# Writing out the whole issue order of an attention and ELU-MLP kernel, in half-pair steps

## The chip, the cores and the metric

The kernel runs on one core of a Trainium2 chip. A core has a matrix engine (TensorE, "PE" in the profile, with its weight loads shown apart as "PEld"), a vector engine (VectorE, "DVE"), a scalar engine (ScalarE, "ACT"), GpSimd ("POOL") and an engine that here issues most DMAs (SyncE, "SP"). Each engine works through its own queue in order. The metric is device time in microseconds (us), less is better; before the change the median of three runs is 621.48 us (619.19 to 624.78). A profile is one execution; its span leaves out a little at both ends.

## The reference

Attention is a gated linear recurrence over 768 tokens, for 4 batches and 8 heads of 48; its output, heads side by side (3072 tokens of 384), goes through a two-layer MLP with ELU.

```python
q, k, v, f_logit: (4, 8, 768, 48) float32;  w_in: (384, 2048), w_out: (2048, 384) float64

f = 1 / (1 + exp(-f_logit))
for t in range(768):
    state = f[t][:, None] * state + outer(k[t], v[t])      # per batch and head, 48 x 48
    y[t] = q[t] @ state
x = y, heads next to each other                            # (3072, 384)
h = x @ w_in
g = where(h > 0, h, exp(min(h, 0)) - 1)
out = g @ w_out
```

The weights come as float64, since a float32 array times a NumPy scalar gives float64. The kernel turns them into float32 itself.

## The kernel before, in words

**Units.** The 3072 tokens are cut into 12 units (`NU`) of 256 tokens, three per batch. For each unit the kernel does the attention and then the MLP. The MLP of unit m and the attention of unit m+1 run side by side. `fast` is the function that runs here; `general` (line 17) is a slower way for extreme gate values, entered at the end only if a flag asks for it (line 949).

**Attention.** A unit is cut into four chunks of 64 tokens. `gates` (545) takes the exponential of the negated gate logits on ScalarE and adds 1, and has GpSimd put restart values at chunk starts. `growth` (557) runs a scan on VectorE per pair of heads, which gives the running product of 1/f, and multiplies k by it on GpSimd. `decays` (569) takes the reciprocal on VectorE and multiplies q by it. A unit has four pairs of heads, so four times scan, reciprocal and product. `transposed` (595) transposes k on TensorE, `advance` (634) computes what each chunk adds to the state, with `stepped` (603) carrying the state over on VectorE; `scores` (614) is q times k within chunks, masked on VectorE; `outputs` (651) multiplies scores by v; `carried` (670) adds q times the state, and has six small DMAs on SP move the fourth pair's rows into the gaps of the other three (694), after which the tile `xt` holds the unit's x.

**MLP.** 2048 hidden columns are 16 blocks (`NFT`) or 8 pairs (`NP`). `up` (783) does a pair: 12 instructions on TensorE into a two-buffer PSUM tile `psH`, relu and exp on ScalarE, and the ELU's last step on VectorE (797). `down` (809) multiplies by w_out. In units 0 and 1 (`DIRECT`) it does so directly, with 8 instructions of 384 columns (818). From unit 2 on it is a Winograd scheme of 7 products of 2x2 blocks instead of 8: 14 instructions of 192 columns (840), four sums of the activations per pair on VectorE (807), and at the end of the unit a few additions on VectorE (850) and one DMA out (857). The sums of weight blocks that the scheme needs are made once by `combine` (771), after unit 0.

**Weights.** Each of 16 parts (768 KB; a pair's columns of w_in, or its rows of w_out) is fetched by `fetch` (470) into one of seven slots of `area`, and made float32 by integer arithmetic: `rounding` (487) on ScalarE scales the low words into a rounding term, in place, and `convert` (495) does three operations on VectorE: shift and mask of the high words into `bits` (508), an integer add of the rounding term (512), and a combination with sign and top exponent bits that writes the float32 tile (518). Later the weights are read once more and `check` (527) takes minimum and maximum (536), for the flag.

**Order.** The opening and unit 0 are issued in the order of the program text (`manual_schedule`, 426). After unit 0 `start.close()` (935) ends that, and for units 1 to 11 the framework's scheduler orders the instructions of each engine by its own costs. Within a unit, the loop at 915 goes over 16 half-pairs: even ones do an up, odd ones the down of the pair before. `attention` (759) hangs TensorE's parts for the next unit on half-pairs 3, 6, 8, 10 and 12 (one later in unit 0), and `prepare` (582) gives one piece of gates, growth or decays per half-pair, so all of a unit's attention is prepared within the unit before it.

Of the kernel before, what the change touches and what calls it, by code (L numbers as in the profile page):

```python
# [10 lines left out]
U32 = mybir.dt.uint32  # L11
AF = mybir.ActivationFunctionType
# [343 lines left out]
def fast(ctx: ExitStack, tc: tile.TileContext, q, k, v, f_logit, w_in, w_out, out, flag):  # L356
# [14 lines left out]

# [17 lines left out]
    DIRECT = 2  # L389
    AHEAD = 7  # L390
# [35 lines left out]
    start.enter_context(tc.manual_schedule())  # L426
    blank(0, nc.vector, nc.gpsimd)
    load(0, nc.scalar)

    ident = cst.tile([128, 128], FP32, name="ident")  # L430
# [14 lines left out]
    for i in range(1, NB):  # L445
        blank(i, nc.gpsimd)
    between = cst.tile([128, NW, HP], FP32, name="between")
    fine = cst.tile([128, HP, NC], FP32, name="fine")
    nc.vector.memset(fine[:], 1.0)
    py = ps.tile([128, HP, W], FP32, tag="a1", name="psY")  # L450
    nc.vector.memset(py[:], 0.0)
# [3 lines left out]
    wi = cst.tile([128, NKT, DFF], FP32, name="wi")  # L455
# [11 lines left out]
    parts = [(0, 0), *((j + i, 1 - i) for j in range(NFT // 2 - 1) for i in (1, 0)), (NFT // 2 - 1, 1)]  # L467

    def fetch(n):
# [4 lines left out]
        to = wo[:, 2 * j : 2 * j + 2] if out_ else wi[:, :, c]  # L474
# [12 lines left out]
    def rounding(n):  # L487

        if wide and n < NFT:
            raw = raws[n]  # L490
            nc.scalar.activation(
                raw.bitcast(I32)[:, 0::2], raw.bitcast(U32)[:, 0::2], AF.Copy, scale=2.0**-29
            )

    def convert(n):

# [3 lines left out]
        j, out_ = parts[n]  # L503
        raw = raws.pop(n)
        rnd = raw.bitcast(I32)[:, 0::2]
        hi = raw.bitcast(I32)[:, 1::2]
        bits = sb.tile([128, 2 * DM], I32, tag="bits", name=f"bits{n}", bufs=1)
# [4 lines left out]
        nc.vector.tensor_tensor(out=bits[:], in0=bits[:], in1=rnd, op=ALU.add)  # L512
        to = wo[:, 2 * j : 2 * j + 2] if out_ else wi[:, :, j * 256 : (j + 1) * 256]
# [3 lines left out]

        nc.vector.scalar_tensor_tensor(
# [7 lines left out]

    def check(n):

        if not wide:
            return  # L530
        w = w_out if n % 2 else w_in
        flat = w.rearrange("a b -> (a b)").rearrange("(p i f) -> i p f", p=128, f=2 * DM)
        raw = area[:, 4 + n % (AHEAD - 4)]
        nc.sync.dma_start(out=raw, in_=flat[n // 2])
        for i, op in enumerate((ALU.min, ALU.max)):
            nc.vector.tensor_reduce(  # L536
                out=spans[:, i, n : n + 1], in_=raw.bitcast(FP32)[:, 1::2], axis=mybir.AxisListType.X,
                op=op, apply_absolute_value=True,
            )


    restart = cst.tile([128, HP, U], FP32, name="restart")
    nc.gpsimd.memset(restart[:], 0.0)

    def gates(u):

        f = qkf[u % NB]["f"]
        pts[u] = sb.tile([128, HP, U], FP32, tag="p", name=f"p{u}")
        for i in range(2):
            a = f[:, 2 * i : 2 * i + 2] if u else f[:, :, i * W : (i + 1) * W]  # L550
            nc.scalar.activation(a, a, AF.Exp, scale=-1.0)
            nc.scalar.activation(a, a, AF.Copy, bias=1.0)
            if u:
                nc.gpsimd.tensor_copy(restart[:, 2 * i : 2 * i + 2, ::C], a[:, :, ::C])
                nc.gpsimd.memset(a[:, :, ::C], 0.0)  # L555

    def growth(u, pairs, cols):

        t = qkf[u % NB]
        for p in range(pairs.start, pairs.stop):  # L560
            a = t["f"][:, p, cols]
            nc.vector.tensor_tensor_scan(  # L562
                out=a, data0=a, data1=restart[:, p, cols] if u else a,
                initial=1.0, op0=ALU.mult, op1=ALU.max,
            )
        k_ = t["k"][:, pairs, cols]
        nc.gpsimd.tensor_tensor(out=k_, in0=k_, in1=t["f"][:, pairs, cols], op=ALU.mult)  # L567

    def decays(u, pairs, cols):

        t = qkf[u % NB]
        nc.vector.reciprocal(pts[u][:, pairs, cols], t["f"][:, pairs, cols])  # L572
        q_ = t["q"][:, pairs, cols]
        nc.vector.tensor_tensor(out=q_, in0=q_, in1=pts[u][:, pairs, cols], op=ALU.mult)
# [7 lines left out]
    def prepare(u):  # L582

        gates(u)
        yield
        for i in range(2):
            for p in range(2 * i, 2 * i + 2):
                growth(u, slice(p, p + 1), slice(0, U))
            yield
        for p in range(HP):  # L590
            decays(u, slice(p, p + 1), slice(0, U))
            yield
        watch(u)

    def transposed(u, w, bank):

        pt = ps.tile([128, HP, 128], FP32, tag=bank, name=f"psT{u}_{w}")
        for p in range(HP):
            nc.tensor.transpose(pt[:, p, :], in_=qkf[u % NB]["k"][:, p, w * W : (w + 1) * W], identity=ident[:])  # L599
        kns[u, w] = sb.tile([128, HP, 128], FP32, tag="kn", name=f"kn{u}_{w}")  # L600
        nc.scalar.copy(kns[u, w][:], pt[:])

    def stepped(u, c, pu, end):

        s = sb.tile([128, HP, D], FP32, tag="state", name=f"state{u}_{c}", bufs=6)
        now = pu
        if u % UPB or c:
# [375 lines left out]
```

## Time and profile before

| | |
|---|---|
| runs | 619.19, 621.48, 624.78 us |
| profiled execution | 622.88 us, its span 620.9 us, mean granted clock of TensorE 0.966 |
| busy: TensorE, VectorE, ScalarE, GpSimd | 572.7, 413.4, 196.7, 59.1 us |
| first up-projection begins, last down ends | 33.9 us, 611.8 us |
| DMA moved | 50.78 MB, 187 to 261 GB/s in most slices of the first 60 us |

How to read the lines that follow. A line of groups gives the kernel's line, engine, operation, what is written and read, the shape, the count, then the busy sum in us and the mean of one in ns, then the idle time before it with what ended that. A line of the timeline gives start and length in us; instructions that follow each other closely are merged, with their count. The chain of waits is the series of pieces of work that led to the last instruction. The row PEclk, where it is shown, is the clock that TensorE was granted, in tenths.

### The profile page before, as it was taken

The page shows a single profiled execution, that of the slowest core. Times are in us where ns is not written, and L with a number is a line of the kernel's source. Part 1 is how long each engine was busy: PE and PEld are TensorE (multiplying, and loading weights), DVE is VectorE, ACT ScalarE, POOL GpSimd, SP SyncE. Part 2 cuts the span into 40 slices and gives each one's busy share as a digit, 9 for nine tenths or more (in the row PEclk, how much of TensorE's full clock was granted, in tenths as well). Part 3 has the DMA queues.
Part 4 walks back from the last instruction along what each step waited for, and adds up shares of the span by engine and source line. Part 5 has one row for each costly group of instructions (what it writes and reads, how often), then busy time and mean ns, then how long its engine had stood idle before and what let it go on. Part 6 is the DMA issues. An engine that isn't in the chain of part 4 may idle for free.

```text
span 620.9 us, 13009 instructions
## 1 busy us (share of the span) xinstructions
PE 572.7 (92%) x5402; PEld 499.3 (80%) x5402; DVE 413.4 (67%) x839; ACT 196.7 (32%) x352; POOL 59.1 (10%) x115
## 2 busy tenths in 40 slices
PE   2787699898999899999999999999999999999994
PEld 1556476675879899899999899999989989999993
DVE  6879999998699976667576675483493443532432
ACT  2254244233413323325314322323313313323220
POOL 7021003223001001002002001000000000000000
PEclk9887799979999999999999999999999999999998
DMA  8999709338682403003112112002000000000000
GB/s 187 250 253 246 184 3 197 64 84 261 221 279 79 159 32 87 26 26 86 44 28 69 41 27 59 27 26 59 25 2 8 26 2 8 26 3 8 27 0 31
DMA packets 31781, 50.78 MB, mean 82 GB/s; under 512 B 3520, under 2 KB 24544, under 8 KB 31712
## 3 DMA queue, kind: packets, MB, share of 16 engines
q1 hardware_dynamic: 31088, 49.26, 30.0%
q8 instruction: 44, 0.72, 0.5%
q10 hardware_dynamic: 624, 0.59, 0.4%
q14 instruction: 25, 0.20, 0.1%
HBM read 44.04 MB, written 4.72 MB: 79 GB/s over the span
## 4 chain that ended last, share of the span: by engine, by line
PE 69%; DVE 14%; DMA 8%; issue 5%; POOL 1%; ACT 1%; SPq 0%; DVEq 0%; POOLq 0%
PE psH L790 33%; PE psM L840 25%; DMA area<-in_moe_w_in_dram 5%; DVE p L572 4%; PE psM L818 3%; DVE f L562 3%; DMA q<-in_q_dram 2%; PE psS L624 2%; DVE spans L536 2%; PE psU_a L643 2%; DVE gg L797 2%; PE psY L661 1%; PE psT L599 1%; PE psY L681 1%; DMA f<-in_f_logit_dram 1%
## 5 line engine op out<-in xcount | busy, mean ns | idle before, releaser
L790 PE MATMUL psH<-xt,wi 128*128 128x256 f32 x1152 | 275.2, 390 | 0.0
L790 PEld LDWEIGHTS psH<-xt,wi 128*128 128x128 f32 x1152 | 218.8, 194 | 32.2
L797 DVE SCALAR_TENSOR_TENSOR gg<-gg,psH 128x512 f32<-128x512 f32 x96 | 64.8, 676 | 162.5 <-ACT gg L796 132.4
L795 ACT ACTIVATE gg<-psH 128x512 f32<-128x512 f32 x96 | 57.2, 596 | 323.6 <-PE psH L790 299.2
L840 PE MATMUL psM<-area,sums 128*128 128x192 f32 x480 | 91.3, 326 | 0.0
L572 DVE RECIPROCAL p<-f 128x256 f32<-128x256 f32 x48 | 82.5, 1734 | 0.3
L840 PEld LDWEIGHTS psM<-area,sums 128*128 128x128 f32 x480 | 80.2, 190 | 0.0
L840 PE MATMUL psM<-wo,gg 128*128 128x192 f32 x320 | 65.5, 327 | 3.5 <-DVE gg L797 3.5
L840 PEld LDWEIGHTS psM<-wo,gg 128*128 128x128 f32 x320 | 55.4, 190 | 8.3 <-DVE gg L797 4.7
L567 POOL TENSOR_TENSOR k<-k,f 128x256 f32<-128x256 f32 x48 | 39.7, 853 | 230.0 <-DMA k<-in_k_dram 196.0
L796 ACT ACTIVATE gg<-gg 128x512 f32<-128x512 f32 x96 | 60.6, 631 | 2.6
L818 PE MATMUL psM<-wo,gg 128*128 128x384 f32 x128 | 47.3, 516 | 3.3 <-DVE gg L797 3.3
L807 DVE TENSOR_TENSOR sums<-gg 128x128 f32<-128x128 f32 x160 | 42.5, 306 | 2.0
L818 PEld LDWEIGHTS psM<-wo,gg 128*128 128x128 f32 x128 | 25.3, 203 | 19.4 <-DVE gg L797 4.1
L562 DVE TENSOR_TENSOR_SCAN f<-f,restart 128x256 f32<-128x256 f32 x44 | 31.6, 761 | 11.6 <-POOL f L555 11.6
L840 PE MATMUL psM<-area,gg 128*128 128x192 f32 x160 | 39.1, 326 | 0.0
L840 PE MATMUL psM<-wo,sums 128*128 128x192 f32 x160 | 39.1, 326 | 0.0
L599 PE MATMUL psT<-ident,k 128*128 128x128 f32 x96 | 15.3, 298 | 18.3 <-POOL k L567 18.3
L536 DVE TENSOR_REDUCE spans<-area 128x1 f32<-128x768 f32 x32 | 29.3, 942 | 2.0 <-DMA area<-in_moe_w_out_dram 1.7
L599 PEld LDWEIGHTS psT<-ident,k 128*128 128x128 f32 x96 | 12.0, 151 | 21.3 <-POOL k L567 20.0
L840 PEld LDWEIGHTS psM<-area,gg 128*128 128x128 f32 x160 | 28.1, 190 | 0.1
L840 PEld LDWEIGHTS psM<-wo,sums 128*128 128x128 f32 x160 | 28.1, 190 | 0.0
(79 smaller groups left out, 427.5 us busy)
## 6 DMA issues: line engine op xcount, KB each, us to landing
area<-in_moe_w_out_dram SPq DMA_DIRECT2D x16, 768.0 KB, 7.7
area<-in_moe_w_in_dram SPq DMA_DIRECT2D x8, 768.0 KB, 5.9
v<-in_v_dram SPq DMA_DIRECT2D x12, 384.0 KB, 4.4
area<-in_moe_w_in_dram SPq DMA_DIRECT2D x16, 288.0 KB, 9.0
f<-in_f_logit_dram SPq DMA_DIRECT2D x23, 192.0 KB, 4.3
k<-in_k_dram SPq DMA_DIRECT2D x23, 192.0 KB, 3.9
q<-in_q_dram SPq DMA_DIRECT2D x23, 192.0 KB, 3.6
out_dram<-o SPq DMA_DIRECT2D x10, 384.0 KB, 2.5
```

The source lines that it names most:

```text
L536: nc.vector.tensor_reduce(out=spans[:, i, n : n + 1], in_=raw.bitcast(FP32)[:, 1::2], axis=mybir.AxisListType.X, op=op, apply_absolute_val ...
L562: nc.vector.tensor_tensor_scan(out=a, data0=a, data1=restart[:, p, cols] if u else a, initial=1.0, op0=ALU.mult, op1=ALU.max,)
L567: nc.gpsimd.tensor_tensor(out=k_, in0=k_, in1=t["f"][:, pairs, cols], op=ALU.mult)
L572: nc.vector.reciprocal(pts[u][:, pairs, cols], t["f"][:, pairs, cols])
L599: nc.tensor.transpose(pt[:, p, :], in_=qkf[u % NB]["k"][:, p, w * W : (w + 1) * W], identity=ident[:])
L790: nc.tensor.matmul(ph[:, i], lhsT=wi[:, kt, n : n + 128], rhs=xts[m][:, kt, :], start=(kt == 0), stop=(kt == NKT - 1),)
L795: nc.scalar.activation(g[:], ph[:], AF.Relu, scale=-1.0)
L796: nc.scalar.activation(g[:], g[:], AF.Exp, scale=-1.0)
L797: nc.vector.scalar_tensor_tensor(out=g[:], in0=g[:], scalar=-1.0, in1=ph[:], op0=ALU.add, op1=ALU.max)
L807: nc.vector.tensor_tensor(out=s[:, i], in0=x, in1=y, op=op)
L818: nc.tensor.matmul(pm[t][:], lhsT=g[:, i, t * 128 : (t + 1) * 128], rhs=wo[:, 2 * j + i, :], start=(j == 0 and i == 0), stop=(j == NP - 1 ...
L840: nc.tensor.matmul(pm[bank][:, half * DH : (half + 1) * DH], lhsT=x, rhs=y, start=first, stop=(j == NP - 1), skip_group_check=True,)
```

## The change

The whole program, not only its start, is issued in the order of the program text, and that order comes from a plan: a table that hangs work on steps, where step T = 16m+s is half-pair s of unit m.

- **Plan of attention.** For unit u with t = 16(u-1): gates at t-8, one pair of heads' decays (scan, reciprocal and both products together) at t-6, t-4, t-2 and t, transposes at t+2, advance and state steps t+4, scores and mask t+6, outputs t+8, carried t+10. Units 1 and 2 have steps of their own.
- **Down two pairs behind.** `down(P - 2)` instead of `down(P - 1)`; the ELU's last step on VectorE becomes `elu`, issued at the start of the next even step.
- **Conversion in two halves.** `split` comes four steps ahead, `merge` two. For parts 3 to 15 `split` masks the high words in place and ScalarE writes its rounding term into their low half, so that `merge` is a single add. w_in lies in eight tiles, one for each pair.
- **combine** is done in unit 1, one operation a step. The second reading of the weights is spread over units 3 to 11, its DMA six steps ahead of the check.
- **Start.** The activation table is loaded at once; dummy matmuls (`warm`) run on TensorE between the first steps; unit 0's attention uses the common functions, with padded copies of v and states that write the fourth pair into the gaps directly; clearing of tiles moves between VectorE and GpSimd.
- **End.** Products of the Winograd scheme are reordered so that bank 2 is last, and a unit's output leaves in four DMAs, in the last unit on two queues.

```diff
     start.enter_context(tc.manual_schedule())
+    nc.scalar.preload_act_table(AF.Exp)
     blank(0, nc.vector, nc.gpsimd)
     load(0, nc.scalar)
...
-    wi = cst.tile([128, NKT, DFF], FP32, name="wi")
+    wi = [cst.tile([128, NKT, 256], FP32, name=f"wi{j}") for j in range(NP)]
...
-    parts = [(0, 0), *((j + i, 1 - i) for j in range(NFT // 2 - 1) for i in (1, 0)), (NFT // 2 - 1, 1)]
+    parts = [(j, 0) for j in range(LAG)] + [(j + i, i == 0) for j in range(NP - LAG) for i in (LAG, 0)]
+    parts += [(j, 1) for j in range(NP - LAG, NP)]
...
+    def split(n):
...
+        bits = held[n] = sb.tile([128, 2 * DM], I32, tag="bits", name=f"bits{n}")
         nc.vector.tensor_scalar(
             out=bits[:], in0=hi, scalar1=3, scalar2=0x3FFFFFF8,
             op0=ALU.logical_shift_left, op1=ALU.bitwise_and,
         )
...
+        if n in SPLIT:
+            nc.vector.tensor_scalar(out=hi, in0=hi, scalar1=-(2**30), scalar2=None, op0=ALU.bitwise_and)
+            rounding(n, over=True)
+
+    def merge(n):
...
+        if n in SPLIT:
+            nc.vector.tensor_tensor(out=to.bitcast(I32), in0=rows(bits[:]), in1=rows(hi), op=ALU.add)
+            return
+        nc.vector.tensor_tensor(out=bits[:], in0=bits[:], in1=lo, op=ALU.add)
         nc.vector.scalar_tensor_tensor(
...
+    def decays(u, p):
 
         t = qkf[u % NB]
-        for p in range(pairs.start, pairs.stop):
-            a = t["f"][:, p, cols]
+        g = t["f"][:, p]
+        for c in range(1 if u or p else NC):
+            a = g if u or p else g[:, c * C : (c + 1) * C]
             nc.vector.tensor_tensor_scan(
-                out=a, data0=a, data1=restart[:, p, cols] if u else a,
-                initial=1.0, op0=ALU.mult, op1=ALU.max,
+                out=a, data0=a, data1=restart[:, p] if u or p else a, initial=1.0, op0=ALU.mult, op1=ALU.max
             )
-        k_ = t["k"][:, pairs, cols]
-        nc.gpsimd.tensor_tensor(out=k_, in0=k_, in1=t["f"][:, pairs, cols], op=ALU.mult)
-
-    def decays(u, pairs, cols):
-
-        t = qkf[u % NB]
-        nc.vector.reciprocal(pts[u][:, pairs, cols], t["f"][:, pairs, cols])
-        q_ = t["q"][:, pairs, cols]
-        nc.vector.tensor_tensor(out=q_, in0=q_, in1=pts[u][:, pairs, cols], op=ALU.mult)
+        nc.vector.reciprocal(pts[u][:, p], g)
+        for e, x, y in ((nc.gpsimd, t["k"], g), (nc.vector, t["q"], pts[u][:, p])):
+            e.tensor_tensor(out=x[:, p], in0=x[:, p], in1=y, op=ALU.mult)
...
+    def attention(u, first, then):
+
+        kept = []
+        for p, i in enumerate(first):
+            at_step(i, lambda p=p: decays(u, p))
+        at_step(first[-1], lambda: watch(u))
+        at_step(then[0], lambda: transposed(u, 0, "a0"), lambda: transposed(u, 1, "a1"))
+        at_step(then[1], lambda: advance(u), *(lambda c=c: step(u, c) for c in range(NC)))
+        at_step(then[2], lambda: kept.append(scores(u)))
+        at_step(then[2], lambda: mask(u, kept[0]))
+        at_step(then[3], lambda: outputs(u))
+        at_step(then[4], lambda: carried(u))
...
         for bank, half, x, y in (
-            (0, 0, a[0][0], b[0][0]), (3, 0, a[0][1], b[1][0]), (2, 1, a[1][1], c[3]),
-            (1, 0, s[:, 0], c[0]), (1, 1, s[:, 2], c[2]), (0, 1, s[:, 1], c[1]), (2, 0, s[:, 3], b[1][1]),
+            (0, 0, a[0][0], b[0][0]), (3, 0, a[0][1], b[1][0]), (0, 1, s[:, 1], c[1]),
+            (1, 0, s[:, 0], c[0]), (1, 1, s[:, 2], c[2]), (2, 1, a[1][1], c[3]), (2, 0, s[:, 3], b[1][1]),
         ):
...
+    pw = ps.tile([128, 128], FP32, tag="m3", name="psW")
+
+    def warm(n):
+
+        for _ in range(n):
+            nc.tensor.matmul(pw[:], lhsT=ident[:], rhs=ident[:], start=True, stop=True)
...
+    warm(20)
+    for p in range(HP):
+        decays(0, p)
+        if p % 2:
+            transposed(0, p // 2, f"m{p // 2}")
+        if p < HP - 1:
+            warm(9)
+        if p < 3:
+            rounding(p)
...
+    pc = scores(0, ("m2", "m3"))
+    advance(0)
+    split(0)
+    split(1)
+    mask(0, pc)
     first_outputs(0)
...
+    for c in range(NC - 1):
+        step(0, c)
...
     first_outputs(1)
...
+    merge(0)
+    gates(1)
+    merge(1)
+    split(2)
+    step(0, NC - 1)
     watch(0)
...
+    split(3)
+    for n in range(NFT):
+        at_step(n, lambda n=n: (merge(n + 2), split(n + 4)))
+    attention(1, (1, 3, 5, 6), (7, 8, 10, 12, 14))
+    attention(2, (16, 18, 19, 20), (22, 24, 26, 28, 30))
+    weights = combine()
+    for n in range(NFT):
+        at_step(NFT + n, lambda: next(weights))
+    at_step(12, lambda: gates(2))
+    for u in range(3, NU):
+        t = (u - 1) * NFT
+        at_step(t - 8, lambda u=u: gates(u))
+        attention(u, (t - 6, t - 4, t - 2, t), (t + 2, t + 4, t + 6, t + 8, t + 10))
...
+    for T in range(NU * NFT):
+        m, s = divmod(T, NFT)
+        P = T // 2
+        if s % 2 == 0 and P:
+            elu(P - 1)
+        for f in plan.pop(T, ()):
+            f()
+        if s % 2 == 0:
+            up(P)
+        elif P >= LAG:
+            down(P - LAG)
...
+    elu(NU * NP - 1)
+    for P in range(NU * NP - LAG, NU * NP):
+        down(P)
+    start.close()
```

More of the change, by code (lines that the diff above doesn't have):

```diff
@@ L580, in watch @@
         )
[L582 to L601, printed above, removed]
```

323 lines of the change are left out of this document (146 added, 177 removed).

## The prediction

> **What bounds the kernel now.** First the page: the span, and the busy share of each engine.
>
> ```profile
> span 620.9 us, 13009 instructions
> PE 572.7 (92%) x5402; PEld 499.3 (80%) x5402; DVE 413.4 (67%) x839; ACT 196.7 (32%) x352; POOL 59.1 (10%) x115
> ```
>
> TensorE binds over the whole. Second, therefore, the busy times by stage (after the stretch: its length, then PE, PEld, DVE, ACT, POOL, the granted clock, DMA share, GB/s). The stretches are: up to the first up-projection, unit 0, unit 1, unit 2, three late units.
>
> ```profile
> 0.00:34.00 34.00, 17.68 (x145) 12.56 (x145) 23.80 (x35) 8.68 (x13) 12.65 (x27) 0.89 0.99 222
> 34.00:99.30 65.30, 53.38 (x425) 38.74 (x424) 60.64 (x89) 27.25 (x45) 7.11 (x12) 0.88 0.70 164
> 99.30:157.00 57.70, 51.76 (x418) 37.60 (x417) 54.73 (x74) 21.79 (x41) 17.55 (x32) 0.91 0.62 159
> 157.00:202.00 45.00, 43.66 (x427) 38.29 (x426) 38.62 (x69) 14.57 (x28) 3.69 (x8) 0.96 0.59 189
> 517.00:562.00 45.00, 45.00 (x474) 41.30 (x473) 18.64 (x53) 13.17 (x25) 0.00 (x0) 1.00 0.04 12
> ```
>
> In late units TensorE is full and VectorE 41% busy. In units 0 and 1 VectorE is 93% and 95% busy and TensorE's clock sags: there VectorE is the bound. Third, what TensorE's work takes when nothing holds it, from the chain of waits (start, length, what): a direct down and an up, then an up and a Winograd down.
>
> ```profile
> 55.35 2.58 PE psM L818 x8
> 57.93 2.59 PE psH L790 x12
> 435.53 2.59 PE psH L790 x12
> 438.12 2.27 PE psM L840 x14
> ```
>
> A pair costs 5.18 where down is direct (a half-pair step 2.59), else 4.86. Fourth, the TensorE timeline (start, length, ..., idle before and its releaser).
>
> ```profile
> 33.94 6.74 PE L790 MATMUL psH<-xt,wi 128*128 128x256 f32 x24
> 51.55 3.80 PE L790 MATMUL psH<-xt,wi 128*128 128x256 f32 x12
> 99.65 5.34 PE L790 MATMUL psH<-xt,wi 128*128 128x256 f32 x24
> 125.14 1.84 PE L624 MATMUL psS<-q,k 48*64 48x64 f32 x38 [1.71 <-DVE state L608]
> 159.59 2.74 PE L818 MATMUL psM<-wo,gg 128*128 128x384 f32 x8
> 406.04 1.15 PE L643 MATMUL psU_a<-v,kn 64*64 64x48 f32 x64
> 450.93 1.15 PE L643 MATMUL psU_a<-v,kn 64*64 64x48 f32 x64
> 611.27 0.49 PE L840 MATMUL psM<-wo,sums 128*128 128x192 f32 x2
> ```
>
> The same instruction group of two units in a row lies 450.93-406.04 = 44.89 apart: 8x4.86 = 38.9 of pairs, so 6.0 of attention. A direct unit without gaps would take 8x5.18+6.0 = 47.4. Laid along the run: the first up is at 33.9; unit 0 lasts to 99.6, 65.7 (18.3 of gaps); unit 1 with its last down to 162.3, 62.7 (15.3 of gaps, such as the bracket, a wait for VectorE); units 2 to 11 need 9x44.89+38.9 = 442.9 and take 611.8-162.3 = 449.5 (6.6 of gaps); then a tail of 620.9-611.8 = 9.1. Gaps are 40 in all.
>
> **The change, part by part.** The prices: groups on VectorE (shape, count, busy us, mean ns of one), then GpSimd's product, DMA landings in the chain, and the first scan.
>
> ```profile
> L423 DVE MEMSET f<- 128x512 f32 x1 | 0.5, 485 | 1.0 <-PEq L965 1.0
> L508 DVE TENSOR_SCALAR bits<-area 128x768 int32<-128x768 int32 x16 | 9.8, 611 | 0.1
> L512 DVE CUSTOM_DVE_ANT_0 bits<-area,bits 128x1536 uint16<-128x1536 uint16 x16 | 16.0, 1002 | 3.2 <-ACT area L491 1.9
> L518 DVE SCALAR_TENSOR_TENSOR wi<-area,bits 128x768 int32<-128x768 int32 x8 | 7.7, 957 | 0.3
> L562 DVE TENSOR_TENSOR_SCAN f<-f,restart 128x256 f32<-128x256 f32 x44 | 31.6, 761 | 11.6 <-POOL f L555 11.6
> L572 DVE RECIPROCAL p<-f 128x256 f32<-128x256 f32 x48 | 82.5, 1734 | 0.3
> L574 DVE TENSOR_TENSOR q<-q,p 128x256 f32<-128x256 f32 x48 | 21.2, 448 | 0.3
> L797 DVE SCALAR_TENSOR_TENSOR gg<-gg,psH 128x512 f32<-128x512 f32 x96 | 64.8, 676 | 162.5 <-ACT gg L796 132.4
> L608 DVE TENSOR_TENSOR state<-psU_a,state 128x192 f32<-128x192 f32 x37 | 13.1, 354 | 3.5 <-PE psU_a L643 2.0
> L629 DVE TENSOR_TENSOR at<-psS,twice 128x512 f32<-128x512 f32 x22 | 14.1, 680 | 0.9 <-PE psS L624 0.9
> L779 DVE TENSOR_TENSOR area<-wo 128x384 f32<-128x384 f32 x8 | 4.3, 552 | 0.1
> L807 DVE TENSOR_TENSOR sums<-gg 128x128 f32<-128x128 f32 x160 | 42.5, 306 | 2.0
> L567 POOL TENSOR_TENSOR k<-k,f 128x256 f32<-128x256 f32 x48 | 39.7, 853 | 230.0 <-DMA k<-in_k_dram 196.0
> 24.71 10.40 DMA area<-in_moe_w_in_dram
> 7.89 0.74 DVE L562 TENSOR_TENSOR_SCAN f<-f 128x128 f32<-128x128 f32 x2 [4.73 <-ACT f L552]
> ```
>
> *Conversion.* A weight part costs 0.61+1.00+0.96 = 2.57 now. In parts 3 to 15 the third operation gives way to a mask of the high words, done two steps earlier, which writes every second word; the merge is the custom add alone. No row shows that mask: it lies between 0.61 (one input, same elements, dense output) and 0.96 (two inputs). I take 0.61, since it has one input: split 1.22, merge 1.00. [...] Added wait: ScalarE's rounding now comes behind VectorE's mask, and relu and exp of that step's up stand behind the rounding; VectorE wants their result two steps later, which covers it.
>
> *Start.* The table load leaves the chain, but VectorE clears more before its first scan: three tiles of 512 columns as now, four of 1024 (restart and three of unit 1, twice 0.49) and two small ones in PSUM, 1.5+3.9+0.8 from 1.0 on. The first scan moves from 7.89 to 7.2. Four pairs of scan, reciprocal and product follow, each D = 0.76+1.73+0.45 = 2.94 (the first 0.1 more): 19.0. Two splits 1.2, two masks of scores 1.4, states with copies 2.1: 23.7. Then VectorE waits for the first outputs on TensorE (72 matmuls at 1.15 for 64, handovers: 1.6) and copies them, 0.5: 25.8. Two full merges 3.9 (the first lets the first up begin, near 28), a split 0.6, state step and watch 0.9, split 1.2: VectorE begins step 0 at 32.4. The 47 dummies (94 instructions at half of 2.59/12) take 10 at full clock, 20 at half, in a TensorE that waits for VectorE from 3 to 19: nothing, or up to 2.5 if the last nine hold up the transposes; I take nothing.
>
> *Unit 0.* Parts arrive every 3.4 (three in 10.40); part n+4, split in step n, is in by 31+3.4n, and VectorE is later than that throughout. In TensorE's order the transposes of unit 1 stand in step 7 and wait for the last scan, in step 6, and GpSimd's product after it; downs and ups behind them wait too. Until that scan VectorE has merges 1.96+6x1.00, splits 7x1.22, elus 3x0.68, 3 D and a scan 0.76: 28.1, so 60.5; the product 0.85: 61.4. Then TensorE owes nine half-pairs and all of the attention, 9x2.59+6.0 = 29.3. It comes from a wait of some 8 us; the up at 51.55, after such a wait, took 3.80 for 2.59, so 1.2 more: 91.9. (VectorE's score mask in step 10 ends at 77.3, TensorE wants it at 78.9: covered, by 1.6.)
>
> [...]
>
> *Unit boundary.* Unit 1's attention is carried out in step 14 instead of 13, unit 2's in 14 of its unit instead of 12; six DMAs on SP's queue must land before the next up. As now (and, for the tail, the last addition):
>
> ```profile
> 559.15 1.11 PE L681 MATMUL psY<-q,state 48*48 48x64 f32 x64
> 561.51 3.67 SPq L694 DMA_DIRECT2D xt<-xt  x6
> xt<-xt SPq DMA_DIRECT2D x66, 16.0 KB, 1.8
> 613.83 0.26 DVE o L850
> ```
>
> From 560.3 to 565.2+1.8 is 6.7; an up and a down cover 5.2. So TensorE waits 1.5, twice: unit 1 begins at 93.4.
>
> *Unit 1.* Combine comes here, one 0.55 a step. Its dense stretch, steps 16 to 20, holds 4 D, 5x0.55 and 3 elus, 16.5; the last scan and product in it end at 14.3+0.85, the transposes come after six half-pairs, 15.5. Covered by 0.3; without that cover, up to 1. So 93.4+47.4+1.5 = 142.3.
>
> *Later.* Two direct downs are still owed, 5.2, then 442.9. A decay pair costs VectorE 0.68+4x0.31+2.94 = 4.9, TensorE 4.86; state steps (7x0.35), score masks and reductions (a pair per unit from unit 3, the rest in 10 and 11) fall in pairs that attention lengthens or that have no decays. The final additions of a unit make VectorE wait for a down in step 3, with an elu behind them, which the lag of two covers. So the 6.6 goes too: TensorE ends at 590.4. Downs 93 to 95 bring no new work.
>
> *Tail.* With bank 2 last, the additions that ran from 611.8 to 614.1 mostly start four matmuls (1.3) earlier: 1.0 saved, and 0.2 for smaller writes on two queues (0 to 0.5, an estimate without a row). 9.1 becomes 7.9. w_in in eight tiles: nothing, since ups ran beside later conversions already.
>
> *Sum.* Span 590.4+7.9 = 598.3; with the 2.0 around the span (622.88) 600.3; the median of the runs is 1.4 below the profiled one: **599**.
>
> **The rivals.**
>
> *VectorE keeps unit 0 longer.* Masks at 0.96 (7x0.35 = 2.5 before step 7), and collisions with GpSimd such as the split below, 0.4 over its mean beside a product; ten of them, 4. Together 605. The row speaks for it; against it, products now fall beside the reciprocal. The last row is for the next rival.
>
> ```profile
> 43.67 1.02 DVE L508 TENSOR_SCALAR bits<-area 128x768 int32<-128x768 int32 x1
> 102.72 3.33 DVE L572 RECIPROCAL p<-f 128x256 f32<-128x256 f32 x2
> ```
>
> [...]
>
> *Less waiting than I count.* The six DMAs land in time (3.0), the clock stays up (1.2), and operations follow closer than their means (two reciprocals in 3.33, not 3.47: 0.07 each, some 50 of them 3.5): 591.
>
> *The written order stalls in the long run.* TensorE waits 1 to 2 us in each of nine units where a decay pair has 4.9 against 4.86: 608 to 617, say 612. Against: two downs of slack, and lengthened pairs right behind.
>
> *Slower.* VectorE becomes the bound of all units. There are 36 decay pairs in nine units; 22 lost makes 0.6 each, which with the 0.4 or so that slack absorbs means D near 4.0; at 4.2 it is 599+36x0.8 = 628. For: the scan's longer cases beside GpSimd. Against: 761, 1734 and 448 are means that contain such company.
>
> *The change doesn't shorten unit 0*, only unit 1: 621-15 = 606, inside the cases above.
>
> **How the numbers follow.** Forecast 0.50 (593 to 606), VectorE longer 0.18, less waiting 0.15, long-run stalls 0.12, slower 0.05. The range of 8 in 10 is 589 to 611. A measurement here tells about 1% from no change: 615.3 and 627.7. Faster: the first three and half the fourth, 0.89; slower most of the fifth, 0.04; 0.07 between.
>
> **What would show it.** The first up near 28; TensorE waiting before the transposes of unit 1 until near 61, on GpSimd's product; unit 1's first up near 93, behind the xt DMAs; units 2 to 10 at 44.9; TensorE's end near 590; a tail under 8.5; mask rows near 0.6. It is wrong if units 2 to 10 take over 45.5, or if VectorE has gaps in steps 0 to 6.

## The result, and the profile after

| | before | changed |
|---|---|---|
| median of the runs, side by side | 622.30 us (619.19 to 624.78, 4 runs) | 604.78 us (603.46 to 605.38, 4 runs) |
| ratio, 95% interval | | 0.9718 (0.9669 to 0.9767) |
| again on another chip | 622.46 us (9 runs) | 605.46 us, ratio 0.9719 (0.9689 to 0.9750) |

The changed kernel is 2.8% faster; 599 was forecast, with 589 to 611. The sum was 5.4 us short in the span (598.3 against 603.7), and the terms that missed lie in the first 70 us. The head of the page of the changed kernel, with the row of the granted clock:

```profile
span 603.7 us, 13549 instructions
PE 570.3 (94%) x5656; PEld 502.7 (83%) x5656; DVE 419.4 (69%) x849; ACT 215.1 (36%) x356; POOL 51.2 (8%) x118
...
PEclk9767699999999999999999999999999999999998
```

TensorE's clock is under nine tenths only in slices two to five of 40, and in the last. By stage (length, busy time of PE, PEld, DVE, ACT, POOL, clock, DMA share, GB/s): the opening, unit 0, unit 1, unit 2, and the last 44.9 before TensorE's end.

```profile
0.00:36.20 36.20, 23.75 (x398) 22.10 (x398) 25.39 (x41) 10.36 (x19) 10.89 (x31) 0.81 1.00 221
36.20:99.70 63.50, 50.12 (x409) 35.71 (x409) 51.35 (x79) 39.81 (x42) 5.59 (x12) 0.84 0.61 150
99.70:147.50 47.80, 47.80 (x426) 35.03 (x426) 36.13 (x55) 16.25 (x29) 5.72 (x11) 1.00 0.21 45
147.50:192.40 44.90, 44.90 (x441) 38.65 (x441) 26.32 (x58) 16.30 (x29) 3.53 (x8) 1.00 0.40 86
551.20:596.10 44.90, 44.89 (x245) 41.80 (x243) 28.79 (x70) 10.49 (x19) 0.00 (x0) 1.00 0.19 63
```

From 99.7 on TensorE has no idle time left. To compare with before, two downs are still owed at 99.7 and at 147.5 (2 x 2.59 = 5.2). So unit 0 with its last down would end at 104.9 instead of 99.6, which is 5.3 lost (2.3 in the opening, 3.0 in unit 0). For unit 1 the kernel before needs care: the 62.7 up to its last down at 162.3 hold the first up of unit 2 as well.

```profile
157.00 2.75 PE L790 MATMUL psH<-xt,wi 128*128 128x256 f32 x12
```

Without that up, 2.6 long, unit 1 took 60.1 and takes 47.8 now, 12.3 won. Units 2 to 11 with it took 452.1 and take 596.1-152.7 = 443.4, 8.7 won; the tail takes 7.6 instead of 9.1, 1.5 won. Together 17.2, the difference of the spans. All of the gain comes after unit 0, and the stretch up to there gives part of it back. This is the opening, first TensorE's timeline (advance, first outputs, first up, and further on the transposes of unit 1 with what follows them):

```profile
23.81 1.53 PE L656 MATMUL psU_a<-v,kn 64*64 64x48 f32 x48 [3.47 <-ACT kn L608]
28.52 1.19 PE L731 MATMUL psY<-q,state 48*48 48x64 f32 x23 [0.46 <-ACT between L738]
31.40 0.67 PE L731 MATMUL psY<-q,state 48*48 48x64 f32 x13 [1.69 <-issue]
32.00 1.49 PE L731 MATMUL psY<-q,padded_s 48*32 48x64 f32 x36
...
67.54 0.69 PE L604 MATMUL psT<-ident,k 128*128 128x128 f32 x2 [5.07 <-POOL k L591]
68.02 5.33 PE L818 MATMUL psM<-wo,gg 128*128 128x384 f32 x8
73.52 1.62 PE L656 MATMUL psU_a<-v,kn 64*64 64x48 f32 x64 [0.17 <-ACT kn L608]
...
99.69 3.05 PE L785 MATMUL psH<-xt,wi 128*128 128x256 f32 x12
```

Then VectorE (the two splits, the first state, the copy of x, the first instruction of step 0) and ScalarE (the rounding of part 2 and, behind it, the copy to kn, the transposed k that the advance reads):

```profile
19.17 2.48 DVE L517 TENSOR_SCALAR bits<-area 128x768 int32<-128x768 int32 x2
25.39 0.36 DVE L622 TENSOR_TENSOR state<-psU_a,p 128x192 f32<-128x192 f32 x1 [2.55 <-PE psU_a L656]
33.67 0.56 DVE L743 COPY xt<-psY 64x384 f32<-64x384 f32 x1 [5.89 <-PE psY L731]
40.26 0.95 DVE L540 CUSTOM_DVE_ANT_0 bits<-area,bits 128x1536 uint16<-128x1536 uint16 x1
```

```profile
22.40 0.89 ACT L509 ACTIVATE area<-area 128x768 int32<-128x768 uint32 x1 [3.52 <-DMA area<-in_moe_w_in_dram]
23.19 0.57 ACT L608 COPY kn<-psT 128x512 f32<-128x512 f32 x1
```

Read them together. ScalarE works in order: the rounding of part 2 was issued ahead of the second kn copy, so the copy, whose transposes were done at 18.3, stood behind a DMA until 23.19. TensorE's advance waited 3.47 for it, VectorE 2.55 for the advance, then 5.89 for the first outputs. Those ran at a low granted clock (0.50 from 28.5 to 33.5; 1.49 for 36 records, that is matmul instructions in the trace, where three of the kernels below take 0.86) and had a pause of 1.69 marked "issue", in which TensorE waited for nothing that the profile shows.

### The profile page after: what moved, and what is told of

Its sections match the earlier page's. It is cut to its first block, busy times and chain, and to the rows that moved or that the text cites. A ratio compares the mean times of both kernels' runs of the same rounds, so it can differ in the third digit from the quotient of the medians.

```text
span 603.7 us, 13549 instructions
## 1 busy us (share of the span) xinstructions
PE 570.3 (94%) x5656; PEld 502.7 (83%) x5656; DVE 419.4 (69%) x849; ACT 215.1 (36%) x356; POOL 51.2 (8%) x118
## 4 chain that ended last, share of the span: by engine, by line
PE 86%; DMA 7%; DVE 5%; issue 1%; SPq 0%; ACT 0%; DVEq 0%
PE psH L785 41%; PE psM L840 30%; PE psM L818 6%; DMA area<-in_moe_w_in_dram 3%; PE psS L635 2%; PE psY L672 2%; PE psU_a L656 2%; PE psY L692 2%; DVE p L589 1%; PE psT L604 1%; DMA q<-in_q_dram 1%; DMA area<-in_moe_w_out_dram 1%; DMA f<-in_f_logit_dram 1%; DVE f L586 1%; DVE wi L538 0%
## 5 line engine op out<-in xcount | busy, mean ns | idle before, releaser
L785 PEld LDWEIGHTS psH<-xt,wi 128*128 128x128 f32 x1152 | 215.5, 192 | 40.6 <-DVE gg L797 6.8
L589 DVE RECIPROCAL p<-f 128x256 f32<-128x256 f32 x48 | 84.2, 1753 | 1.7
L591 POOL TENSOR_TENSOR k<-k,f 128x256 f32<-128x256 f32 x48 | 35.0, 728 | 209.5 <-DVE f L586 200.6
L807 DVE TENSOR_TENSOR sums<-gg 128x128 f32<-128x128 f32 x160 | 39.5, 288 | 2.7
L850 DVE TENSOR_TENSOR o<-psM,u 128x192 f32<-128x192 f32 (+1 forms) x30 | 11.8, 421 | 38.4 <-ACT u L851 38.0
L509 ACT ACTIVATE area<-area 128x768 uint16<-128x768 uint32 (+1 forms) x16 | 27.9, 1742 | 28.2 <-DVE area L522 16.5
```

The lines of the kernel that those rows point to most:

```text
L509: nc.scalar.activation(to, raw.bitcast(U32)[:, 0::2], AF.Copy, scale=2.0**-29)
L589: nc.vector.reciprocal(pts[u][:, p], g)
L591: e.tensor_tensor(out=x[:, p], in0=x[:, p], in1=y, op=ALU.mult)
L785: nc.tensor.matmul(ph[:, i], lhsT=wi[j][:, kt, i * 128 : (i + 1) * 128], rhs=xts[m][:, kt, :], start=(kt == 0), stop=(kt == NKT - 1),)
L807: nc.vector.tensor_tensor(out=s[:, i], in0=x, in1=y, op=op)
```

## The experiments

Each kernel is the changed one with the edit shown, except where the kernel before is named. Ratios are to the kernel before on the same chip.

**ScalarE's queue.** Is it the rounding in front of the kn copy that holds the opening?

```diff
-        if p < 3:
+        if p < 2:
             rounding(p)
+    rounding(2)
```

> The changed kernel with the rounding of part 2 moved on ScalarE's queue behind the copy of unit 0's second transposes. Theory Q (queues of the opening): in the changed kernel that copy stands behind a rounding that waits for a DMA until 22.4, and TensorE's advance, VectorE's state steps and the first merge (34.2) follow it; moved, the copy starts near 18.5, the first merge comes 3 to 5 us earlier, and since VectorE is without gaps from there to step 7, the time falls by 3 to 5 us, from 604.8 to about 601. Rival D (DMA): the weight parts' arrival sets unit 0; VectorE starts earlier but gets gaps in steps 0 to 6 of the same size, and the time stays within 1 us.

Measured: 602.61, ratio 0.9718 (0.9674 to 0.9761). TensorE's timeline:

```profile
19.94 1.22 PE L656 MATMUL psU_a<-v,kn 64*64 64x48 f32 x64
28.27 0.43 PE L731 MATMUL psY<-q,state 48*48 48x64 f32 x13 [2.54 <-issue]
32.44 7.15 PE L785 MATMUL psH<-xt,wi 128*128 128x256 f32 x24 [2.74 <-DVE wi L541]
95.89 3.05 PE L785 MATMUL psH<-xt,wi 128*128 128x256 f32 x12
```

The wait for kn is gone, and in the trace the first up and unit 1's first up both begin 3.8 earlier. The ratio is the changed kernel's to the last digit, with an interval of ±0.4%, where 3.8 would be 0.6%. So the trace shows the queue as the cause of the wait; what it is worth in time this run alone does not settle. The wait moves with the landing of part 2: in the profiles of the kernels that leave this part of the opening as it is, it is 1.74 to 4.81, and the first up begins anywhere from 33.20 to 37.88. The 32.44 here lies under that range by only 0.8.

**VectorE's merges behind the first outputs.** They need nothing of the outputs, but stand behind the copy that waits for them.

```diff
-    first_outputs(1)
     merge(0)
-    gates(1)
     merge(1)
+    first_outputs(1)
+    gates(1)
```

> The changed kernel with the merges of parts 0 and 1 issued ahead of the second half of unit 0's first outputs, so that VectorE does them in its gap of 5.9 us (27.8 to 33.7). Theory Q: two merges of 1.9 leave the stretch behind the gap, step 0 begins 3.8 us earlier, and the time falls by 3 to 4 us, to about 601. Rival D: no change, since parts 4 to 10 arrive no earlier.

Measured: 601.32, ratio 0.9686 (0.9642 to 0.9731). VectorE's and TensorE's timelines:

```profile
33.09 0.56 DVE L743 COPY xt<-psY 64x384 f32<-64x384 f32 x1 [0.86 <-PE psY L731]
```

```profile
95.41 3.03 PE L785 MATMUL psH<-xt,wi 128*128 128x256 f32 x12
```

The wait of 5.89 became 0.86, and unit 1's first up came 4.3 earlier, with a wait for kn as long as in the changed kernel (3.51). In the trace, then, what VectorE loses in the opening does reach unit 1; the interval of the ratio overlaps the changed kernel's.

**The transposes of unit 1 two steps later.** They make TensorE wait 5.07 in step 7; would it not rather do downs and ups meanwhile?

```diff
-    attention(1, (1, 3, 5, 6), (7, 8, 10, 12, 14))
+    attention(1, (1, 3, 5, 6), (9, 10, 11, 13, 14))
```

> The changed kernel with unit 1's transposes in step 9 instead of 7, advance in 10, scores in 11, outputs in 13, carried in 14. Theory T (TensorE's order): from 59.8 to 67.5 TensorE stands in step 7 although a down and an up are ready; they now run in that wait, 2.6 us each, and the clock stays up (in the changed kernel the down behind the wait took 5.3 instead of 2.6): unit 1's first up comes 4 to 7 us earlier than 99.7, and the time falls by as much, to 598 to 601. Rival V: VectorE's later work (state steps, score mask, merges to 15) is the true bound of unit 0, so TensorE only waits later: within 1.5 us.

Measured: 606.55, ratio 0.9774 (0.9733 to 0.9814). TensorE's timeline, then ScalarE's:

```profile
76.01 2.43 PE L656 MATMUL psU_a<-v,kn 64*64 64x48 f32 x64 [6.99 <-ACT kn L608]
```

```profile
73.64 1.89 ACT L509 ACTIVATE area<-area 128x768 uint16<-128x768 uint32 x1
75.29 1.15 ACT L608 COPY kn<-psT 128x512 f32<-128x512 f32 x2
```

The expected gain is not there: the wait moved. The kn copies now stand behind more roundings, which themselves wait for VectorE's masks, and TensorE waits 6.99 in one place. Unit 1's first up begins at 99.50, as in the changed kernel, but the first up began at 33.20 already: between the two lie 66.3 instead of 63.5, so unit 0 became 2.8 longer.

**Dummies ahead of those transposes**, to keep the clock up (12 before the first half, 20 before the second).

```diff
     def transposed(u, h, bank):
+        if u == 1:
+            pw1 = ps.tile([128, 128], FP32, tag="m2", name=f"psX{h}")
+            for _ in range(12 if h == 0 else 20):
+                nc.tensor.matmul(pw1[:], lhsT=ident[:], rhs=ident[:], start=True, stop=True)
```

> The changed kernel with dummy matmuls ahead of unit 1's two groups of transposes (24 and 40 instructions, 2.6 and 4.3 us at full clock), which fill TensorE's wait in step 7. Theory C (clock): after the wait of the changed kernel the down took 5.3 instead of 2.6 and the advance 1.6 instead of 1.15; with the clock kept up these 3 us go, less up to 1 us by which dummies run over: time down by 2 to 3 us, to 602 to 603. Rival: the clock recovers by itself at no cost to the end, or dummies hold the transposes up: within 1 us, or slower by 1 to 3.

Measured: 607.57, ratio 0.9786 (0.9746 to 0.9826).

```profile
68.87 2.75 PE L822 MATMUL psM<-wo,gg 128*128 128x384 f32 x8
74.53 0.31 PE L660 MATMUL psU_a<-v,kn 64*64 64x48 f32 x2 [2.92 <-ACT kn L612]
76.08 4.54 PE L789 MATMUL psH<-xt,wi 128*128 128x256 f32 x12
```

The down behind the wait took 2.75 instead of 5.33, and nothing was won: TensorE then waited 2.92 for the kn copies, and the next up took 4.54, where it takes 2.86 in the second run of the changed kernel below (75.17). From the first up (37.26) to unit 1's (102.39) it is 65.1, 1.7 longer than in the changed kernel. So the low clock (0.50 from 67.5 to 73 in the changed kernel) wasn't the only bound there. In the changed kernel the slow down hides the lateness of kn almost exactly (0.17 of wait).

**The changed kernel again**, as the measure for three kernels on its chip.

> The changed kernel once more, on the chip of the three kernels that follow, as their measure: 604.8 within 1.5, the ratio to the kernel before 0.972 within 0.004. Its first up pass should begin between 33 and 38 and unit 1's first between 96.5 and 101, as the landing of the third part of the weights (L509's wait before the kn copies) shifts from run to run.

Measured: 605.46 (604.39 to 605.93). The first up is at 36.37, the last transposes at 67.66, unit 1's first up at 99.80. Here the down took 3.98 and the wait for kn was 1.49, with the same end.

**Both at once**: the dummies, and unit 1's transposes and kn copies issued ahead of the merge and rounding of step 7.

```diff
+    at_step(7, lambda: transposed(1, 0, "a0"), lambda: transposed(1, 1, "a1"))
     for n in range(NFT):
         at_step(n, lambda n=n: (merge(n + 2), split(n + 4)))
...
-        at_step(then[0], lambda: transposed(u, 0, "a0"), lambda: transposed(u, 1, "a1"))
+        if u > 1:
+            at_step(then[0], lambda: transposed(u, 0, "a0"), lambda: transposed(u, 1, "a1"))
```

> The dummies of the warm-up before unit 1's last transposes, as in the earlier run, but now the transposes and the two kn copies are issued ahead of the merge and the rounding of step 7, so that ScalarE copies kn at about 69.1 in the scale of the changed kernel instead of 72.8. Theory Q2 (ScalarE's queue and the cold clock share the stretch from 68 to 74, and only both together give it back): the down of step 7 takes about 2.7 instead of 5.3, the advance follows it at about 71.3 instead of 73.5 and does not wait for kn, and unit 1's first up comes 2 to 3 earlier than in the changed kernel relative to its own first up: first up to unit 1's first up 60.5 to 61.5 against 63.45. Time about 2.3 less. Rival V (VectorE has no room left, since its own stretch is full to 73.7): states begin at 73.7 and what follows is bound by VectorE; distance 62.5 to 63.5, time within 1 of the changed kernel.

Measured: 602.08 (600.66 to 603.33), ratio 0.9662 (0.9632 to 0.9692).

```profile
37.88 7.09 PE L790 MATMUL psH<-xt,wi 128*128 128x256 f32 x24 [2.75 <-DVE wi L541]
69.44 2.75 PE L823 MATMUL psM<-wo,gg 128*128 128x384 f32 x8
72.11 1.15 PE L660 MATMUL psU_a<-v,kn 64*64 64x48 f32 x64
97.82 3.05 PE L790 MATMUL psH<-xt,wi 128*128 128x256 f32 x12
```

From the first up to unit 1's first up it is 97.82-37.88 = 59.94, against 99.80-36.37 = 63.43: 3.5 less, and 3.4 less in the time. Clock and ScalarE's queue held the same stretch, and both together give it back. The dummies alone made it longer; the kn copies alone were not moved, but in the kernel without the second mask, further on, they come at once without dummies, and the part behind the transposes is only 0.9 shorter.

**All three edits that helped** (rounding, merges, and the last one).

> Three edits together: the third rounding behind the kn copies of unit 0, the first two merges ahead of the second half of unit 0's outputs, and for unit 1 the kn copies first with the dummies ahead of the transposes. If the losses of the opening and of the stretch after step 7 are separate, they add: VectorE's step 0 about 6.5 earlier (3.8 for the queue, the rest of its 5.9 gap for the merges), unit 1's first up at 90.5 to 93 instead of 99.7, TensorE full behind it, time 596 to 598.5. If the two edits of the opening share one loss (both end where TensorE's own states and outputs end), unit 1's first up comes at 93 to 95.5 and the time is 598.5 to 601.

Measured: 597.85 (596.55 to 598.79), ratio 0.9594 (0.9563 to 0.9626): 1.3% under the changed kernel beside it, with no run of the one in the range of the other, and the fastest of all. Unit 1's first up, and VectorE's last waits ahead of it in unit 0:

```profile
92.59 3.06 PE L790 MATMUL psH<-xt,wi 128*128 128x256 f32 x12
```

```profile
34.59 0.95 DVE L540 CUSTOM_DVE_ANT_0 bits<-area,bits 128x1536 uint16<-128x1536 uint16 x1
...
37.20 0.56 DVE L517 TENSOR_SCALAR bits<-area 128x768 int32<-128x768 int32 x1 [0.67 <-DMA area<-in_moe_w_in_dram]
...
40.70 0.56 DVE L517 TENSOR_SCALAR bits<-area 128x768 int32<-128x768 int32 x1 [1.48 <-DMA area<-in_moe_w_out_dram]
```

Step 0 begins at 34.59, 2.2 behind the forecast's 32.4. The two edits of the opening don't add in full: alone they bring step 0 forward by 3.8 and 4.3, together by 5.7. VectorE still waits 2.68 for the first outputs, in which TensorE's pause was 3.51 here, and then overtakes the weights and waits 2.15 for their DMAs. Unit 1's first up is 7.2 earlier, the time 7.6 less, both within what was expected for separate losses.

**The two halves of the conversion.** The form of parts 0 to 2 for all 16: no mask, rounding to 32 bits as its data land, two merging instructions.

```diff
-    SPLIT = range(3, NFT)
+    SPLIT = range(0)
...
+        elif n > 2:
+            rounding(n)
```

> All sixteen parts of the weights go through the form that parts 0 to 2 have: no second mask, a rounding to 32 bits (0.9 each instead of 1.93) that waits for its DMA alone, and two merging instructions (0.95 and 0.96) instead of one. Theory V (VectorE alone sets unit 0 up to step 7): by the last scan of unit 1 six merges cost 0.96 more each and eight second masks of 0.56 are gone, so 5.8 less 4.5 or 1.3 later at that scan, and by the end of step 7 some 2 to 2.5; unit 1's first up counted from unit 0's first is 1.3 to 3 later than in the changed kernel, time 1 to 3 more. Theory S (the 1.93 roundings on ScalarE and their waits for the masks are what holds the kn copies and TensorE): the kn copies come at once, and the distance is 1 to 3 shorter, time 1 to 3 less.

Measured: 604.87 (603.54 to 605.76), ratio 0.9711 (0.9680 to 0.9743): no difference. Both effects appear and cancel. From its first up (35.20) to its last transposes (67.68) it is 32.48 against 31.29, 1.2 longer on VectorE as worked out; behind them TensorE doesn't wait for kn, and from there to unit 1's first up it is 31.28 against 32.14.

```profile
68.16 5.17 PE L820 MATMUL psM<-wo,gg 128*128 128x384 f32 x8
73.27 1.15 PE L658 MATMUL psU_a<-v,kn 64*64 64x48 f32 x64
```

**No dummies.** (There are 20+3x9 = 47 of them; the expectation misstates the count.)

> The changed kernel without any of its 56 dummy products of the opening (20, and 9 after each of the first three decays). The forecast took them at nothing, with 0 to 2.5 us of cost as bounds. Theory N (the opening is set by VectorE's decays, then by the landing of the weights and ScalarE's queue; the clock is low again before the kn copies end anyway): first up within 1.5 of 36.4 apart from the landing, distance from it to unit 1's first up 63.4, time within 1 of the changed kernel. Rival W (the dummies keep the clock up for the transposes and scores): these take about twice as long, 1 to 2.5 us more before the kn copies, time 1 to 2.5 more.

Measured: 602.51 (601.83 to 603.77), ratio 0.9697 (0.9664 to 0.9730). First up at 33.31, and from it to unit 1's 63.5 as before. The kn wait was shorter (ScalarE's rounding of part 2 began at 22.18, in the second run of the changed kernel at 23.29), and the pause "issue" was another one:

```profile
28.05 0.47 PE L731 MATMUL psY<-at,padded_v 64*32 64x64 f32 x10 [0.43 <-issue]
28.89 0.88 PE L731 MATMUL psY<-q,state 48*48 48x64 f32 x36 [0.38 <-ACT between L738]
```

From the first up to the last matmul it is 559.4 with and without them, so the dummies bring nothing behind the opening; whether they cost 1 or 2 us in it lies within the intervals.

**The framework's scheduler from unit 1 on.** `start.close()` at the first step of unit 1.

```diff
+        if T == NFT:
+            start.close()
```

> The written order is given up where unit 1's first step begins; from there the framework's scheduler orders the same instructions by its own costs, as it did in the kernel before. Theory M (the order by hand is what took the idle time out of units 1 to 11): TensorE's idle time comes back there, up to 6.6 us in units 2 to 11 as in the kernel before and some in unit 1, time 606 to 618. Rival F (what took it out is that down stands two pairs behind up and the attention is spread over steps, which the scheduler keeps since it starts from the same sequence): TensorE is full from unit 1 on here too, time within 1.5 of the changed kernel.

Measured: 613.30 (611.98 to 614.79), ratio 0.9872 (0.9837 to 0.9907). Two stretches that hold units 1 and 2 (windows), and unit 2's first up (timeline):

```profile
101.00:152.00 51.00, 48.59 (x424) 36.01 (x423) 50.49 (x79) 21.92 (x41) 13.49 (x31) 0.97 0.70 191
152.00:197.00 45.00, 42.90 (x425) 36.84 (x424) 42.70 (x76) 14.66 (x27) 3.61 (x8) 1.00 0.70 225
```

```profile
153.61 2.83 PE L785 MATMUL psH<-xt,wi 128*128 128x256 f32 x12 [1.11 <-DMA xt<-xt]
```

TensorE is idle there for 4.5 (2.4 and 2.1), waiting for VectorE's states and 1.1 for xt; later units are full. Unit 1's first up is at 100.93, so the unit takes 52.7 instead of 60.1 before and 47.8 in the changed kernel: three fifths of what it won is there without the order by hand, which is worth 1.5% by the ratios and 6.7 in the spans. This is what theory M expected.

VectorE shows where it goes. In unit 1 it is busy for 50.49 of 51.00, against 36.13 of 47.80 in the changed kernel. The scheduler issues work of later units early. These are groups on VectorE from 100.93 to 153.61, the scans and the check of the weights' second reading:

```profile
L586 DVE TENSOR_TENSOR_SCAN f<-f,restart 128x256 f32<-128x256 f32 x21 | 14.3, 721 | 0.4 <-POOL f L577 0.4
L561 DVE TENSOR_REDUCE spans<-area 128x1 f32<-128x768 f32 x10 | 9.1, 938 | 0.0
```

The changed kernel has 8 scans and no check in unit 1, the kernel before 20 scans and 8 checks. So the order by hand wins in unit 1 by leaving later work for later, where VectorE has room (busy for 26.32 of the 44.90 of unit 2 in the changed kernel). No run moves these instructions alone.

**The written order alone**, in the kernel before.

```diff
         if m == 0:
-            start.close()
             combine()
...
     down(NU * NP - 1)
+    start.close()
```

> The kernel before with one edit: its instructions stay in the order in which its program writes them to the end, where the scheduler took over behind the opening. Theory M (the written order alone is worth the gain in the later units): the 6.6 of idle time in units 2 to 11 go, time 612 to 617. Theory F (without the steps the written order puts an attention in one block in front of the passes, and TensorE waits for VectorE's decays and masks in every unit): some us more of idle time per unit, time above 625, as far as 700.

Measured: 691.11 (687.22 to 695.85), ratio 1.1112 (1.1060 to 1.1164). TensorE's waits (us, times, longest):

```profile
PE psT L599 <- POOL k L567: 59.9, 41, 11.5
```

A written order that hasn't been spread over steps costs 70 (the waits for GpSimd's product ahead of the transposes alone were 18.3 in the kernel before); the scheduler had been hiding that. It is the plan and the order together that win.

**Down one pair behind up.**

```diff
-    LAG = 2
+    LAG = 1
```

> Down stands one pair behind up instead of two. Between the end of an up and the down that needs its result stand then only the next up (2.7) and two half-steps of attention, and in that time ScalarE's two functions (0.6 each) and VectorE's 0.7 and sums have to be done. Theory G (two pairs are needed): TensorE waits for the sums wherever VectorE has attention work in its queue, and in unit 0 behind the merges, 0.3 to 2 in each of 96 pairs at most, time 612 to 640. Rival H (in the later units VectorE is idle a third of the time and keeps up): only unit 0 is longer, by 0 to 4, time 603 to 609.

Measured: 602.22 (601.11 to 603.58), ratio 0.9687 (0.9654 to 0.9721): not slower. TensorE is full from unit 1 on here too, and unit 0 takes the same time though one more of its downs lies in it:

```profile
35.77:99.20 63.43, 51.26 (x416) 36.42 (x417) 51.27 (x79) 39.75 (x42) 5.55 (x12) 0.89 0.66 147
99.20:147.00 47.80, 47.80 (x426) 35.04 (x426) 36.12 (x55) 16.22 (x29) 5.70 (x11) 1.00 0.21 45
```

The second pair of lag buys nothing in this kernel; the forecast had counted on it for the final additions. From the first up to the last matmul it is 556.9 here, against 559.4 in both profiles of the changed kernel: shorter by about the one down that unit 0 took in. Whether one pair is faster than two in time is left open: the intervals of the ratios overlap.

**Not run.** No kernel takes the early table load, the eight tiles of w_in, the place of combine or the edits of the end away alone, so what each of them is worth is open.

## Why the prediction was right, and where its sum was off

**The step that failed: "VectorE begins step 0 at 32.4".** It was 40.26, 7.9 late, and with it the first up was at 36.24 and not "near 28". Of that, 1.3 is the two splits at 19.17, 2.48 instead of 1.2, the first some 1.9 while GpSimd clears tiles (18.04 to 20.77), the second 0.55; 2.5 is the wait for the advance, which the forecast didn't have, as it did not follow ScalarE's queue (its size moves with the landing of part 2); 4.3 is the first outputs, 5.89 of waiting against the 1.6 taken (1.69 of it the pause "issue", some 2 the clock of 0.50, estimated from 72 records in 3.35 where 64 take 1.15 at a granted clock of 1.00 in the kernel before, 0.7 that the first half was itself late); smaller things give 0.2 back. The runs on the rounding and the merges take these back in the trace, and with the combined kernel step 0 begins at 34.59. The opening's sum took TensorE and ScalarE as free.

**Unit 0 up to the last scan.** Forecast 28.1 from step 0, measured 66.7-40.3 = 26.4, without a gap on VectorE, as forecast. The mask was taken at 0.61 and is 0.564; a scan is 0.684 instead of 0.761. In the kernel before, four scans in a row took 3.40 (at 99.40): 1.20 for the first two, 2.20 for the other two, which began while GpSimd's products were running (100.16 to 104.00); now the products lie beside the reciprocals. On ScalarE the 16-bit rounding doubled, from 903 ns, which the forecast did not price:

```profile
L522 DVE TENSOR_SCALAR area<-area 128x768 int32<-128x768 int32 x13 | 7.3, 564 | 0.5
L586 DVE TENSOR_TENSOR_SCAN f<-f,restart 128x256 f32<-128x256 f32 x47 | 32.1, 684 | 0.0
```

```profile
L509 ACT ACTIVATE area<-area 128x768 uint16<-128x768 uint32 x13 | 25.1, 1933 | 16.5 <-DVE area L522 16.5
```

**From the product to unit 1's first up.** The signs came: TensorE waits before the transposes on GpSimd's product, though until 67.5 and not 61. From there 29.3+1.2+1.5 = 32.0 was forecast, and 32.15 measured, by errors that cancel, which is luck. "1.2 more" for the clock was 3.1 in all: the down took 5.33 for 2.75, with a granted clock of 0.50 from 67.5 to 73, and the advance 1.62 for 1.15, of which the clock explains little (0.96 from 73.52 to 75.14); its first records lie beside the second kn copy (two copies, 72.78 to 73.95). "TensorE waits 1.5, twice" for the xt DMAs was at most 0.3 (the up of 3.05 against 2.75). And six of the eight transposes, some 0.6 of the 6.0 for attention, lay ahead of the wait.

**Unit 1 and later.** 47.4+1.5 was forecast, 47.8 measured; 44.89 a unit, measured 44.9; from the end of unit 1 to TensorE's end 448.1, measured 448.6; the tail 7.9, measured 7.6 (the 0.2 in it for smaller writes on two queues was the author's estimate without a row, and no run shows it by itself). The split of the gaps before was misread (unit 1 with 15.3, the later units with 6.6, where the up at 157.00 makes it 12.7 and 9.2); the sum doesn't rest on it, but the rival's 606 would have been 608. Why the gaps go was argued from VectorE having room; that it has room because the scans and checks of later units no longer come in unit 1 was not in the working. "VectorE has gaps in steps 0 to 6" and "units 2 to 10 over 45.5", which would have made it wrong, did not come.

**The sum of the misses:** +7.9 in the opening, -1.8 on VectorE and GpSimd up to the product (67.5 against 61.4, so +6.1 there), +0.2 from there to unit 1's first up, -1.1 in unit 1 (no second xt wait), +0.5 in the later units, -0.3 in the tail: 5.4.

**The rivals.** "VectorE keeps unit 0 longer" gave 605 and met the time with the wrong mechanism: masks and collisions in unit 0 cost nothing, the stage was shorter. A collision may lie in the opening instead, at the two splits. "Doesn't shorten unit 0" describes it best: unit 0 ends later than before, and the gain lies in the units behind, though not in unit 1 alone. Of "Less waiting than I count" the six DMAs came true, the clock did not. Long-run stalls and the slower case left no trace: units are 44.9 throughout. Costing the dummies and the 16-bit rounding at nothing held in the time, the rounding only because TensorE's down at a clock of 0.50 (5.33) covered what ScalarE was late; the eight tiles are not tested.

## What to carry to other kernels

When steps are moved by hand, follow every engine's queue in order, the lightly loaded ones too: here an instruction that waited for a DMA on an engine 36% busy held the two bound engines. Where two causes end at the same moment, removing either one shows nothing; read what is late next and take both away before calling a cause false. In this kernel a written order paid only with a plan that spreads the work over steps, and the plan paid in full only with the order, which kept later units' work off a full engine.

## What the runs showed of the hardware that was not expected

In all eleven profiles of kernels with the dummies, TensorE pauses 1.6 to 3.5 us in the opening, always after the same instruction, the 23rd record of the q-and-state products. In the combined kernel there are two pauses (0.90 and 3.51), 9+48+48+23 = 128 matmul records apart; with each goes a weight load, so 256 instructions. Without the 47 dummies (94 records) the pause, 0.43 there, lies 33 records earlier, and 94+33 = 127. In the changed kernel the DMA queues from 28 to 31 us show:

```profile
q8 instruction: 1, 0.02, 2.2%
```

The whole page has 46 such packets and 0.75 MB, so some 16 KB each, for 11,312 matmul and weight-load records; the page of the kernel before has 44 for 10,804, which is one for 246 in both. One packet lies in the stretch of the pause, on DMA engines that the weights fill (share 1.00 in the opening). The distance of the two pauses, 256 records, is near the 246 records to a packet. Against it, without the dummies no such packet lies from 27 to 29 us, where the pause of 0.43 is. That the packet is the cause is the author's inference from place and period; no run moved it by itself.

A 16-bit result written into every fourth half-word cost ScalarE 1.93 us for 768 elements, against 0.90 for 32 bits. VectorE's mask with such a stride in 32 bits cost nothing extra (0.564 against 0.557 for the dense split).
